# Whole PSUM pairs for every step of an attention and MLP kernel, and a fixed order per engine in the MLP

## The chip, the cores and the metric

The kernel runs on one core of a Trainium2 chip. The metric is device time in microseconds (us), the median of several executions; lower is better. One more execution of the kernel was profiled, and all rows below come from that one.

The engines are named as in the profile: PE (matrix multiply; PEld is its weight load), DVE, ACT, POOL, and SP, which issues the DMAs.

## The reference

Everything is float32 on the way out; the weights `w_ch1`, `w_ch2`, `U` and `V` of the second half come in as float64.

```python
# attention: batch 4, heads 12, seq 448, head_dim 64
scores = scale * q @ k^T                      # per head
scores = einsum('bhij,hg->bgij', scores, w_pre)    # mix the heads
attn = exp(scores - max); attn = attn / (sum + 1e-9)
attn = einsum('bhij,hg->bgij', attn, w_post)  # mix the heads again
x = (attn @ v) as (4, 448, 768)
# MLP: rank 32, d_ff 3072
h = x^T @ U @ V                               # along the sequence, low rank
u = x + h^T
out = u + max(u @ w_ch1, 0) @ w_ch2
```

## The kernel before

**Attention.** The tokens of a batch are cut into four groups (a unit `u` is one group of one batch, 16 in all), and each unit into chunks of ten tokens, 180 in all, taken in pairs `k`. The steps are `qk` (line 414), `premix` (445), `neg_max`, `exp`, `scale_w`, `postmix` (480), and, twice for each unit, `av` (521, 529). The result is added up in `acc[b]`, which holds batch b transposed: 6 chunks `c` of 128 channels by 448 tokens.

**Low rank.** When a batch is through, `flip` transposes its chunks (709), `flip_h` and `flip_l` take them out of PSUM as a high and a low part, `by_u` multiplies by U (727), `by_v` by V (740), and `add_h` adds the product to `acc[b]` (743). `split_uh` and `split_ul` then make `uh` and `ul`, the two parts of u that the MLP multiplies.

**MLP.** The hidden layer is cut into 24 slices `f` of 128. `up` (782) makes one slice for one batch: 18 matmuls (6 chunks, three products of high and low parts each) into one PSUM bank. `relu_h` (ACT, 787) and `relu_l` (DVE, 791) take it out as `hh` and `hl`. `down` (802) multiplies two slices at once by the second weights, six matmuls for each of the 6 chunks, each chunk into its own bank, and `gather` (DVE, 806) adds the bank to `acc[b]`. So a slice costs 4 x 18 matmuls up and 4 x 6 x 3 down, 144 in all.

**Weights.** Each slice has four pieces of 128x384 float64 words (two of each weight matrix). `piece` loads one (615) into one of two buffers `kr` and narrows it: `abs` (622 on ACT or 624 on DVE), then 629, 633, 634, 638 and 639 on DVE, the sum 643 on POOL or DVE, then the high part (a copy, on ACT, POOL or DVE) and the low part (a subtraction, line 339, on DVE or POOL). Each step is a step of the plan with a list of engines that may take it.

**What sets the order.** `Plan.order` is a list scheduler that runs when the kernel is built: each step has a rank (the table `RANK`), a cost, needs and slots; whenever an engine is free, it takes the ready step of lowest rank whose slots are free. What comes out is the program order of every engine. From slice 2 on (`RANK["even"]`), `plan.line` fixes the order of PE's MLP steps: one `up`, then three `down`s from a queue. The other engines' steps are ordered by rank alone.

**PSUM.** There are 8 banks, made as 4 tiles `BANKS[i]` of two banks each. The steps in `PAIRS` (`qk`, `pre`, `post`, `av`) take both halves of a tile; `lr` (low rank), `up` and `dn` take one half, and the other half may belong to another step at the same time:

```python
def bank(*s):
    w = plan.where[s]
    return BANKS[w[0] // 2] if len(w) == 2 else BANKS[w[0] // 2][:, w[0] % 2]
```

In the listings below the four tiles appear as bank_58 to bank_61, whichever half is meant.

Of the kernel before, what the change touches and what calls it, by code (L numbers as in the profile page):

```python
# [23 lines left out]
NJ = 4  # L24
# [21 lines left out]
class Unit:  # L46
# [11 lines left out]
    m0=7.312, mb=7.238, mf=2.802, e0=-51.192, estep=4.488, er=4.899, ne=8, qk_lead=5.047, qk_step=0.838, av_off=3.874,  # L58
    av_step=1.434, post=4.408, kr=3.969, vr=1.605, qr=5.01, mx=0.769, ex=1.029, ep=2.642, po=1.859, qo=0.493, 
    uv0=6, uvs=1.515, uv1=2.707, u0=0.057, us=8.218, w0=-3.04, w1=17.823, up=-0.049, raw=8, even=2, ga=-0.275, k0=-13.668, kstep=0.83,  # L60
# [3 lines left out]
CAPS = dict(qk=2, pre=3, post=3, av=2, lr=4, up=3, dn=6)  # L64
PAIRS = ("qk", "pre", "post", "av")
# [17 lines left out]
def f32(ap):  # L83
    return ap.bitcast(F32)
# [6 lines left out]
class Plan:  # L91
# [8 lines left out]
    def __init__(self, rings, banked, banks, weight):  # L100
        self.rings = {n: list(range(c)) for n, c in rings.items()}
        self.banked, self.where = banked, {}
        self.bank_free = list(range(banks))
        self.banks = banks
        self.weight = weight
        self.steps = {}
        self.port = {}
        self.users = {}
        self.line = []
# [20 lines left out]

    def fits(self, names):
        free = list(self.bank_free)
        for n in sorted(names, key=lambda n: n not in PAIRS):
            got = self.find(n, free)
            if got is None:
                return False
            for g in got:
                free.remove(g)
        return True

    def take(self, s):
        if s[0] not in self.banked:
            self.where[s] = self.rings[s[0]].pop(0)
            return
        got = self.find(s[0], self.bank_free)
        for g in got:
            self.bank_free.remove(g)
        if s[0] in PAIRS:
            self.pairs_left -= 1
        self.where[s] = got  # L150

    def order(self):
# [8 lines left out]
        self.pairs_left = sum(s[0] in PAIRS for s in self.users)  # L161
# [13 lines left out]
        place = {k: i for i, k in enumerate(self.line)}  # L175
        reached = 0

        def pick(e):
            for r in ready[e]:
                rank, _, k = r  # L180
                if place.get(k, reached) != reached:
                    continue
# [5 lines left out]
                if any(left[n] < c for n, c in need.items()) or not self.fits([n for n, c in need.items() if n in self.banked for _ in range(c)]):  # L188
                    continue
# [12 lines left out]
        while events:  # L202
            now = events[0][0]
            while events and events[0][0] <= now:
# [12 lines left out]
                for s in steps[k][4]:  # L217
                    users[s] -= 1
                    if users[s] == 0:
                        held.discard(s)  # L220
                        if s[0] in self.banked:
                            self.bank_free += self.where[s]
                        else:
                            self.rings[s[0]].append(self.where[s])
# [6 lines left out]
            while moved:  # L231
                moved = False
                for e in free:
# [7 lines left out]
                    reached += k in place  # L241
                    for o, _ in engines:
                        ready[o].remove(r)
                    for s in sorted(slots, key=lambda s: s[0] not in PAIRS):
# [30 lines left out]
def build(tc, q2, kt, vj, wpre_in, wpost_in, u_in, v_in, ident, w1j, w2, out, show=None):  # L275
# [11 lines left out]
    plan = Plan({**BUFS, **CAPS, "t": 2}, CAPS, 8, WEIGHT)  # L287
# [313 lines left out]
    def piece(key, src, n, p, rank, finish, slots, opened, cost, early=None):  # L601
# [57 lines left out]
        plan.add((key, "abs"), [("ACT", 60 + 395 * s), ("DVE", 60 + 210 * s)], narrow0, r0, [(key, 0)], [raw, first_tmp])  # L659
# [3 lines left out]
        plan.add((key, 4), [("POOL", 100 + 900 * s), ("DVE", 60 + 410 * s)], narrow4, r0, [(key, 3)], [first_tmp], port=BOTH)  # L663
# [42 lines left out]
    def flip(eng, b, c):  # L706
        t = T["tp", b, c] = bank("lr", ("tp", b, c))[:JP, :].rearrange("p (j c) -> p j c", j=NJ)
        for j in range(NJ):
            eng.transpose(t[:, j, :], acc[b][:, c, j * JP:(j + 1) * JP], sb["ident"])

    def flip_h(eng, b, c):
        xh = tile_of(("xh", b, c // 2), lambda: sb["xn"].tile([JP, NJ, LW], F32R, "xh", ("xn", (b, c // 2))))
        copy(eng, xh[:, :, c % 2 * 128:c % 2 * 128 + 128], T["tp", b, c])

    def flip_l(eng, b, c):
        xl = tile_of(("xl", b, c // 2), lambda: sb["xn"].tile([JP, NJ, LW], F32R, "xl", ("xn", (b, c // 2))))
        cut = slice(c % 2 * 128, c % 2 * 128 + 128)
        sub(eng, xl[:, :, cut], T.pop(("tp", b, c)), f32(T["xh", b, c // 2][:, :, cut]))

    def by_u(eng, b, k):  # L720
        xh, xl = T.pop(("xh", b, k)), T.pop(("xl", b, k))
        full = T["t1", b, k] = bank("lr", ("tr", b, k))
        ps = full[:, :LW]
        i = 0
        for y in (xl, xh):
            for j in range(NJ):
                eng.matmul(ps, lhsT=sb["u4"][:, j].rearrange("p i r -> p (i r)"), rhs=y[:, j, :], start=(i == 0), stop=(i == 7))
                i += 1

    def t_h(eng, b, k):  # L730
        t3 = T["t3", b, k] = sb["t3"].tile([4 * R, LW], F32R, "t3", ("t3", (b, k)))
        copy(eng, t3, T["t1", b, k][:, :LW])

    def t_l(eng, b, k):
        t3 = T["t3", b, k]
        sub(eng, t3[R:2 * R], T.pop(("t1", b, k))[R:2 * R, :LW], f32(t3[R:2 * R]))

    def by_v(eng, b, c):
        hp = T["hp", b, c] = bank("lr", ("hp", b, c))[:, :S]
        eng.matmul(hp, lhsT=T["t3", b, c // 2][:, c % 2 * 128:c % 2 * 128 + 128], rhs=sb["v4"], start=True, stop=True)  # L740

    def add_h(eng, b, c):
        eng.tensor_tensor(out=acc[b][:, c, :S], in0=acc[b][:, c, :S], in1=T.pop(("hp", b, c)), op=ALU.add)
# [7 lines left out]
    for b in range(B):  # L751
        RB = first[(b + 1) * NG] + RANK["uv0"]
        us = range(b * NG, (b + 1) * NG)
        for c in range(KC):
            k, r = c // 2, RB + RANK["uvs"] * c
            tp, xn = ("lr", ("tp", b, c)), ("xn", (b, k))
            plan.add(("tp", b, c), [("PE", 490)], partial(flip, b=b, c=c), r, ["ident"] + [("av_add", u, c // AV * AV) for u in us], [tp, xn])
            plan.add(("xh", b, c), [("ACT", 482)], partial(flip_h, b=b, c=c), r, [("tp", b, c)], [tp, xn])
            plan.add(("xl", b, c), [("DVE", 601)], partial(flip_l, b=b, c=c), r, [("xh", b, c)], [tp, xn])
        for k in range(KC // 2):  # L760
            r = RB + RANK["uvs"] * (2 * k + 1) + RANK["uv1"]
            tr, t3 = ("lr", ("tr", b, k)), ("t3", (b, k))
            plan.add(("t1", b, k), [("PE", 1450)], partial(by_u, b=b, k=k), r, [(("u",), 6), ("xl", b, 2 * k), ("xl", b, 2 * k + 1)], [tr, ("xn", (b, k))])
            plan.add(("th", b, k), [("ACT", 272)], partial(t_h, b=b, k=k), r, [("t1", b, k)], [tr, t3])
            plan.add(("tl", b, k), [("DVE", 336)], partial(t_l, b=b, k=k), r, [("th", b, k)], [tr, t3])
        for c in range(KC):
            k = c // 2
# [165 lines left out]
```

## Time and profile before

| | |
|---|---|
| median of 3 executions | 1213.48 us (1212.97 to 1216.55) |
| the profiled execution, its own time | 1214.14 us |
| its span, first to last instruction | 1212.3 us |
| PE busy | 1092.5 us, 90% of the span |
| DVE busy | 717.4 us, 59% |
| ACT busy | 379.9 us, 31% |
| POOL busy | 255.9 us, 21% |
| mean granted clock of PE | 0.961 of full speed |

About 1.8 us of the profiled execution's time lie outside its span. Matmuls are pipelined, so a busy share of PE counts overlapping instructions once and says little on its own; what one matmul costs is read from the distance between the starts of neighbours.

### The profile page before, as it was taken

How to read it: one execution, taken by the hardware profiler on the slowest of the kernel's cores; microseconds unless marked ns; L12 is line 12 of the kernel's file. 1: busy time of each engine (PE TensorE's matmuls, PEld its weight loads, DVE VectorE, ACT ScalarE, POOL GpSimd, SP SyncE). 2: the span in 40 equal slices, each digit the busy share in tenths (PEclk: the TensorE clock that was granted, in tenths of full speed). 3: DMA queues.
4: the chain of work that ended last, by engine and by line, in shares of the span. 5: the costliest groups of instructions: out<-in, count | busy, mean ns of one | idle time of the engine just before them, and what ended most of it. 6: DMA issues, size and time to landing. Idle time of an engine off the chain costs nothing.

```text
span 1212.3 us, 28459 instructions
## 1 busy us (share of the span) xinstructions
PE 1092.5 (90%) x12120; PEld 898.5 (74%) x12120; DVE 717.4 (59%) x1308; ACT 379.9 (31%) x811; POOL 255.9 (21%) x390
## 2 busy tenths in 40 slices
PE   4899999998999999988979888897988889798998
PEld 1556665666668888777868887786887778687897
DVE  0665654655887877565556465654646665565535
ACT  2767777677686222101101111110111011110100
POOL 3221111112145034121212121212212221221200
PEclk8999999999999999999989999997988999999899
DMA  7664555456642012111111111111101111111004
GB/s 274 193 195 151 172 184 162 146 157 201 195 147 75 27 52 79 52 53 26 53 49 43 40 52 52 42 37 52 52 27 52 53 40 39 52 53 31 22 1 182
DMA packets 52414, 108.11 MB, mean 89 GB/s; under 512 B 5200, under 2 KB 38464, under 8 KB 51776
## 3 DMA queue, kind: packets, MB, share of 16 engines
q1 hardware_dynamic: 52288, 106.30, 28.8%
q8 instruction: 95, 1.56, 0.5%
q14 instruction: 31, 0.25, 0.1%
HBM read 57.91 MB, written 7.08 MB: 54 GB/s over the span
## 4 chain that ended last, share of the span: by engine, by line
PE 70%; DVE 19%; DMA 4%; issue 3%; ACT 2%; SPq 1%; DVEq 0%; ACTq 0%; POOL 0%
PE bank L782 29%; PE bank L802 19%; PE bank L480 5%; PE bank L445 5%; DVE acc L806 5%; PE bank L414 5%; PE bank L521 5%; DMA t<-s 3%; DVE a L634 3%; DVE x L639 3%; DVE a L633 2%; DVE hl L791 2%; PE bank L529 1%; DVE w1l L339 1%; DVE x L638 1%
## 5 line engine op out<-in xcount | busy, mean ns | idle before, releaser
L782 PE MATMUL bank<-uh,w0l 128*128 128x448 f32 x576 | 227.9, 396 | 72.9 <-DVE acc L806 71.6
L787 ACT ACTIVATE hh<-bank 128x448 fp32r<-128x448 f32 x96 | 52.5, 547 | 647.2 <-PE bank L782 530.5
L806 DVE TENSOR_TENSOR acc<-acc,bank 128x448 f32<-128x448 f32 x300 | 181.2, 616 | 117.6 <-PE bank L782 74.1
L782 PE MATMUL bank<-ul,w0h 128*128 128x448 f32 x576 | 223.0, 387 | 0.0
L782 PE MATMUL bank<-uh,w0h 128*128 128x448 f32 x576 | 222.4, 386 | 0.0
L802 PE MATMUL bank<-hh,w1l 128*128 128x448 f32 x576 | 211.6, 367 | 4.0 <-DVE acc L806 3.0
L802 PE MATMUL bank<-hl,w1h 128*128 128x448 f32 x576 | 211.0, 366 | 0.3 <-DVE hl L791 0.2
L802 PE MATMUL bank<-hh,w1h 128*128 128x448 f32 x576 | 210.8, 366 | 0.0
L782 PEld LDWEIGHTS bank<-uh,w0l 128*128 128x128 f32 x576 | 116.8, 203 | 95.8 <-DVE acc L806 83.5
L643 POOL TENSOR_TENSOR a<-a,x 128x384 f32<-128x384 f32 (+2 forms) x97 | 102.3, 1055 | 392.3 <-DVE x L639 384.8
L791 DVE SCALAR_TENSOR_TENSOR hl<-bank,hh 128x448 fp32r<-128x448 f32 x96 | 59.4, 619 | 201.9 <-ACT hh L787 201.9
L450 DVE TENSOR_REDUCE mx<-bank 128x2 f32<-128x896 f32 x90 | 97.5, 1087 | 76.6 <-PE bank L445 71.5
L782 PEld LDWEIGHTS bank<-uh,w0h 128*128 128x128 f32 x576 | 116.6, 202 | 10.8
L782 PEld LDWEIGHTS bank<-ul,w0h 128*128 128x128 f32 x576 | 117.0, 203 | 10.1
L802 PEld LDWEIGHTS bank<-hh,w1l 128*128 128x128 f32 x576 | 108.1, 188 | 16.0 <-DVE acc L806 5.1
L455 ACT ACTIVATE e<-bank,mx 128x448 f32<-128x448 f32 x180 | 113.2, 639 | 20.8 <-DVE mx L450 11.5
L480 PEld LDWEIGHTS bank<-wr,e 60*64 60x64 f32 x5040 | 90.6, 136 | 37.1 <-issue 27.3
L802 PEld LDWEIGHTS bank<-hl,w1h 128*128 128x128 f32 x576 | 108.2, 188 | 10.0 <-DVE hl L791 0.9
L802 PEld LDWEIGHTS bank<-hh,w1h 128*128 128x128 f32 x576 | 108.2, 188 | 9.2
L414 PE MATMUL bank<-k,q 64*60 64x448 f32 (+1 forms) x768 | 95.3, 563 | 16.4 <-ACT s L332 9.6
L445 PE MATMUL bank<-t,wpre 64*64 64x448 f32 x720 | 90.3, 559 | 10.8 <-DMA t<-s 6.0
L480 PE MATMUL bank<-wr,e 60*64 60x60 f32 x5040 | 94.2, 220 | 6.0 <-issue 4.6
(64 smaller groups left out, 1122.0 us busy)
## 6 DMA issues: line engine op xcount, KB each, us to landing
t<-s SPq DMA_DIRECT2D x192, 210.0 KB
kr<-in_w1j SPq DMA_DIRECT2D x48, 384.0 KB
kr<-in_w SPq DMA_DIRECT2D x48, 384.0 KB
v<-in_vj SPq DMA_DIRECT2D x4, 1536.0 KB
q<-in_q SPq DMA_DIRECT2D x32, 186.0 KB
out<-acc SPq DMA_DIRECT2D x24, 224.0 KB
k<-in_kt SPq DMA_DIRECT2D x4, 672.0 KB
k<-in_kt SPq DMA_DIRECT2D x4, 448.0 KB
```

The costliest lines, as they stand in the source:

```text
L414: eng.matmul(o[at, i, :S], lhsT=q[d, p, at], rhs=k[d, p, :], start=True, stop=True)
L445: eng.matmul(o[64 * j:64 * j + 64, i, :S], lhsT=wpre[64 * i:min(64 * i + 64, QW)], rhs=tt[u % 2][64 * i:min(64 * i + 64, QW), n, :], start ...
L450: eng.tensor_reduce(out=mx, in_=T["pre", k][:, :, :S], axis=AX.X, op=ALU.max, negate=True)
L455: eng.activation(out=e[:, i], in_=T["pre", k][:, i, :S], func=ACTF.Exp, bias=T["mx", k][:, i:i + 1], accum_out=sm[:, i:i + 1])
L480: eng.matmul(d, lhsT=e[64 * j:64 * j + HALF, i, x * KB:x * KB + KB], rhs=wr[64 * j:64 * j + HALF, i].rearrange("p (g m) -> p g m", m=MH), ...
L521: eng.matmul(main[i * D:(i + 1) * D, c, :n], lhsT=v[:, p + c, i, x, :], rhs=a[:, x * H + 2 * (p + c) + i, :n], start=(c == 0 and x == 0), ...
L643: eng.tensor_tensor(out=f32(a), in0=f32(a), in1=f32(x), op=ALU.add)
L782: eng.matmul(ps, lhsT=w[:, c * 128:(c + 1) * 128], rhs=u[:, c, :], start=(i == 0), stop=(i == 3 * KC - 1))
L787: eng.activation(out=hh, in_=T["up", f, b], func=ACTF.Relu)
L791: eng.scalar_tensor_tensor(out=hl, in0=T.pop(("up", f, b)), scalar=0.0, in1=f32(T["hh", f, b]), op0=ALU.max, op1=ALU.subtract)
L802: eng.matmul(ps, lhsT=w[:, cut], rhs=h, start=(i == 0), stop=(i == len(todo) - 1))
L806: eng.tensor_tensor(out=dst, in0=dst, in1=T.pop(("dn", f, b, c)), op=ALU.add)
```

## The change

Every step that uses PSUM now takes a whole tile of two banks. `down`, the transposes and the V products work on two chunks per step, so that both banks are filled; `up` and the U products use the first bank of their tile and leave the second empty. The planner's search for halves (`find`, `fits`, `PAIRS`) goes. In the MLP, from slice 2 on, the order is fixed on four engines (`plan.lines`): for each batch b of slice f, the piece `(w, f + 1, b)` is narrowed, then `hh` and `hl` of `(f, b)`, then one `down` for an even b and two for an odd b, with their `gather`s. For pieces of slices above 2, `abs` and the high part are ACT's alone, the sum and the low part POOL's alone. The ranks are numbers of another search, of which two lines are shown.

```diff
 RANK = dict(
-    m0=7.312, mb=7.238, mf=2.802, e0=-51.192, estep=4.488, er=4.899, ne=8, qk_lead=5.047, qk_step=0.838, av_off=3.874,
+    m0=13.16, mb=7.238, mf=2.802, e0=-51.192, estep=4.488, er=6.178, ne=8, qk_lead=5.047, qk_step=0.838, av_off=4.137,
...
-CAPS = dict(qk=2, pre=3, post=3, av=2, lr=4, up=3, dn=6)
-PAIRS = ("qk", "pre", "post", "av")
+CAPS = dict(qk=2, pre=3, post=3, av=2, lr=2, up=2, dn=3)
...
     def take(self, s):
-        if s[0] not in self.banked:
-            self.where[s] = self.rings[s[0]].pop(0)
-            return
-        got = self.find(s[0], self.bank_free)
...
+        ring = self.bank_free if s[0] in self.banked else self.rings[s[0]]
+        self.where[s] = ring.pop(0)
...
-        place = {k: i for i, k in enumerate(self.line)}
-        reached = 0
+        place = {k: (n, i) for n, line in enumerate(self.lines) for i, k in enumerate(line)}
+        reached = [0] * len(self.lines)
...
-    plan = Plan({**BUFS, **CAPS, "t": 2}, CAPS, 8, WEIGHT)
+    plan = Plan({**BUFS, **CAPS, "t": 2}, CAPS, 4, WEIGHT)
...
     def bank(*s):
-        w = plan.where[s]
-        return BANKS[w[0] // 2] if len(w) == 2 else BANKS[w[0] // 2][:, w[0] % 2]
+        return BANKS[plan.where[s]]
...
-        plan.add((key, "abs"), [("ACT", 60 + 395 * s), ("DVE", 60 + 210 * s)], narrow0, r0, [(key, 0)], [raw, first_tmp])
+        plan.add((key, "abs"), [("ACT", 60 + 395 * s), ("DVE", 60 + 210 * s)][:1 if steady else 2], narrow0, r0, [(key, 0)], [raw, first_tmp])
...
-        plan.add((key, 4), [("POOL", 100 + 900 * s), ("DVE", 60 + 410 * s)], narrow4, r0, [(key, 3)], [first_tmp], port=BOTH)
+        plan.add((key, 4), [("POOL", 100 + 900 * s), ("DVE", 60 + 410 * s)][:1 if steady else 2], narrow4, r0, [(key, 3)], [first_tmp], port=BOTH)
...
-    def down(eng, fs, b, c):
-        cut = slice(c * 128, (c + 1) * 128)
-        ps = T["dn", fs[-1], b, c] = bank("dn", (fs[-1], b, c))[:, :S]
+    def down(eng, fs, b, c, n):
+        ps = T["dn", fs[-1], b, c] = bank("dn", (fs[-1], b, c))
...
-        for i, (w, h) in enumerate(todo):
-            eng.matmul(ps, lhsT=w[:, cut], rhs=h, start=(i == 0), stop=(i == len(todo) - 1))
-
-    def gather(eng, f, b, c):
-        dst = acc[b][:, c, :S]
-        eng.tensor_tensor(out=dst, in0=dst, in1=T.pop(("dn", f, b, c)), op=ALU.add)
...
+        for j in range(n):
+            for i, (w, h) in enumerate(todo):
+                eng.matmul(ps[:, j, :S], lhsT=w[:, (c + j) * 128:(c + j + 1) * 128], rhs=h, start=(i == 0), stop=(i == len(todo) - 1))
+
+    def gather(eng, f, b, c, n):
+        eng.tensor_tensor(out=two(b, c, n), in0=two(b, c, n), in1=T.pop(("dn", f, b, c))[:, :n, :S], op=ALU.add)
...
-                  [(f"w{i // 2}", f)], "open_a" if i > 1 else ("open_qk", "open_mix", "open_a")[min(f, 2)], (HIGH(HW), LOW(HW)), early() if f < 2 else None)
+                  [(f"w{i // 2}", f)], "open_a" if i > 1 else ("open_qk", "open_mix", "open_a")[min(f, 2)], ([("ACT", act(HW))], [("POOL", gps(HW))]) if f > RANK["even"] else (HIGH(HW), LOW(HW)),
+                  early() if f < 2 else None, f > RANK["even"])
...
-                line.append(("up", f, b))
-                line += queue[:3]
-                del queue[:3]
...
+    def some(n):
+        lines["PE"] += [("dn",) + q for q in queue[:n]]
+        lines["DVE"] += [("ac",) + q for q in queue[:n]]
+        del queue[:n]
+
+    for f in range(RANK["even"], KF):
         for b in range(B):
...
+            lines["PE"].append(("up", f, b))
+            key = ("w", f + 1, b)
+            if f + 1 < KF:
+                lines["ACT"].append((key, "abs"))
+                lines["DVE"] += [(key, i) for i in (1, 2, 3)]
+                lines["POOL"] += [(key, i) for i in (4, 6)]
+            lines["ACT"].append(("hh", f, b))
+            lines["DVE"].append(("hl", f, b))
+            if f + 1 < KF:
+                lines["ACT"].append((key, 5))
+            some(1 + b % 2)
+            queue += [(f, b, c) for c in range(KC) if ("dn", f, b, c) in plan.steps]
+    some(len(queue))
```

What this does to PE's order is seen from the tile that each group of matmuls writes. The rows below are the first matmul of each group, from the middle of the MLP of the kernel before; a group of line 802 (a `down`) has 6 matmuls, one of line 782 (an `up`) has 18.

```order
L802 MATMUL bank_61<-hh_6245,w1l_6326 128x448
...
L802 MATMUL bank_58<-hh_6245,w1l_6326 128x448
...
L802 MATMUL bank_60<-hh_6245,w1l_6326 128x448
...
L782 MATMUL bank_58<-uh,w0l_5888 128x448
...
L802 MATMUL bank_61<-hh_6245,w1l_6326 128x448
...
L802 MATMUL bank_60<-hh_6245,w1l_6326 128x448
...
L802 MATMUL bank_59<-hh_6245,w1l_6326 128x448
...
L782 MATMUL bank_59<-uh,w0l_5888 128x448
```

The first `up` goes into tile 58, whose other half the `down` before last has just filled; the second goes into tile 59, whose other half the `down` right ahead of it has filled. In the changed kernel PE's row in the middle of the MLP reads as follows, again the first matmul of each group; a group of line 770 (a `down`) now has 12 matmuls, one of line 750 (an `up`) has 18.

```order
L770 MATMUL bank_58<-hh_6034,w1l_6279 128x448
...
L770 MATMUL bank_61<-hh_6034,w1l_6279 128x448
...
L750 MATMUL bank_60<-uh,w0l_5825 128x448
...
L770 MATMUL bank_59<-hh_6200,w1l_6279 128x448
...
L750 MATMUL bank_58<-uh,w0l_5825 128x448
...
L770 MATMUL bank_61<-hh_6200,w1l_6279 128x448
...
L770 MATMUL bank_60<-hh_6200,w1l_6279 128x448
...
L750 MATMUL bank_59<-uh,w0l_5825 128x448
```

Each tile now comes back after exactly three other groups. The second place is DVE in the same stretch. Before, two pieces are narrowed with their instructions mixed, then `hl` and the `gather`s (`acc`) follow in the order of their ranks:

```order
L633 SCALAR_TENSOR_TENSOR a_5404<-kr_545,a_5404 128x384
L634 SCALAR_TENSOR_TENSOR a_5404<-x_5403,a_5404 128x384
L638 TENSOR_SCALAR x_599<-a_600 128x384
L639 SCALAR_TENSOR_TENSOR x_599<-kr_732,x_599 128x384
L638 TENSOR_SCALAR x_5403<-a_5404 128x384
L639 SCALAR_TENSOR_TENSOR x_5403<-kr_545,x_5403 128x384
L791 SCALAR_TENSOR_TENSOR hl_6079<-bank_59,hh_6051 128x448
L806 TENSOR_TENSOR acc<-acc,bank_61 128x448
L806 TENSOR_TENSOR acc<-acc,bank_58 128x448
L806 TENSOR_TENSOR acc<-acc,bank_60 128x448
L791 SCALAR_TENSOR_TENSOR hl_5990<-bank_58,hh_5978 128x448
```

In the changed kernel DVE's row has one piece, one `hl` (line 759) and one or two `gather`s (line 773), each of two chunks, and then the next piece:

```order
L759 SCALAR_TENSOR_TENSOR hl_5959<-bank_58,hh_5956 128x448
L773 TENSOR_TENSOR acc<-acc,bank_61 128x2x448
L773 TENSOR_TENSOR acc<-acc,bank_60 128x2x448
L596 TENSOR_SCALAR a_600<-kr_765 128x384
L600 SCALAR_TENSOR_TENSOR a_600<-kr_765,a_600 128x384
L601 SCALAR_TENSOR_TENSOR a_600<-x_599,a_600 128x384
L605 TENSOR_SCALAR x_599<-a_600 128x384
L606 SCALAR_TENSOR_TENSOR x_599<-kr_765,x_599 128x384
L759 SCALAR_TENSOR_TENSOR hl_6202<-bank_59,hh_6200 128x448
```

No two pieces stand one behind the other any more, and no `gather` or `hl` reads a tile that another open step shares.

## Rows read from the trace of the kernel before

**Rows 1.** PE in three stretches (stretch, length, busy, instructions, clock, DMA share, GB/s).
```profile
370.33:476.43 106.10, 98.50 (x695) 1.00 0.20 58
476.43:1183.71 707.28, 636.49 (x2932) 0.95 0.15 43
542.34:1102.72 560.38, 500.18 (x2304) 0.95 0.16 46
```

**Rows 2.** The chain that ended last (start, length, what): groups of 18 matmuls.
```profile
683.14 5.50 PE bank L782 x18
688.64 3.65 PE bank L802 x18
...
1144.15 3.72 PE bank L802 x18
```

**Rows 3.** Who waited for whom, whole span (total us, times, longest).
```profile
ACT hh L787 <- DVE acc L806: 114.6, 19, 6.6
DVE acc L806 <- PE bank L782: 74.1, 19, 4.3
PE bank L782 <- DVE acc L806: 71.6, 30, 3.7
```

**Rows 4.** Timeline of one stall: DVE, then ACT, POOL and PE (in brackets: idle before, and its releaser).
```profile
676.21 0.62 DVE L806 TENSOR_TENSOR acc<-acc,bank 128x448 f32<-128x448 f32 x1 [3.70 <-PE bank L782]
680.26 1.23 DVE L639 SCALAR_TENSOR_TENSOR x<-kr,x 128x384 f32<-128x384 uint32 x1
681.41 0.61 DVE L791 SCALAR_TENSOR_TENSOR hl<-bank,hh 128x448 fp32r<-128x448 f32 x1
681.95 1.67 DVE L806 TENSOR_TENSOR acc<-acc,bank 128x448 f32<-128x448 f32 x3
...
680.03 1.04 POOL L643 TENSOR_TENSOR a<-a,x 128x384 f32<-128x384 f32 x1 [11.21 <-DVE x L639]
...
683.14 0.47 PE L782 MATMUL bank<-uh,w0l 128*128 128x448 f32 x1 [3.32 <-DVE acc L806]
```

**Rows 5.** Groups of instructions in the stretch 542.34 to 1102.72 (busy, mean ns, idle before).
```profile
L782 PE MATMUL bank<-uh,w0l 128*128 128x448 f32 x384 | 154.0, 401 | 60.2 <-DVE acc L806 60.2
...
L806 DVE TENSOR_TENSOR acc<-acc,bank 128x448 f32<-128x448 f32 x193 | 116.8, 615 | 84.4 <-PE bank L782 63.8 <-PE bank L802 20.1
...
L802 PEld LDWEIGHTS bank<-hh,w1h 128*128 128x128 f32 x384 | 72.1, 188 | 6.0
...
L643 POOL TENSOR_TENSOR a<-a,x 128x384 f32<-128x384 f32 x64 | 69.1, 1080 | 289.5 <-DVE x L639 289.5
L639 DVE SCALAR_TENSOR_TENSOR x<-kr,x 128x384 f32<-128x384 uint32 x64 | 46.7, 730 | 2.2
L634 DVE SCALAR_TENSOR_TENSOR a<-x,a 128x384 f32<-128x384 f32 x64 | 45.6, 712 | 5.9 <-DVE a L633 0.5
L633 DVE SCALAR_TENSOR_TENSOR a<-kr,a 128x384 int32<-128x384 int32 x64 | 35.4, 553 | 0.5
...
L638 DVE TENSOR_SCALAR x<-a 128x384 int32<-128x384 int32 x64 | 22.5, 352 | 0.0
L629 DVE TENSOR_SCALAR a<-kr 128x384 int32<-128x384 int32 x64 | 21.2, 353 | 0.0
```

**Rows 6.** The group over the whole span in which DVE reads two PSUM banks at once.
```profile
L450 DVE TENSOR_REDUCE mx<-bank 128x2 f32<-128x896 f32 x90 | 97.5, 1087 | 76.6 <-PE bank L445 71.5 <-ACT e L455 4.8
```

**Rows 7.** Timeline: two weight loads of SP's queue, and the ACT step that waited for them.
```profile
437.62 1.85 SPq L615 DMA_DIRECT2D kr<-in_w1j  x2
...
442.49 0.56 ACT L622 ACTIVATE x<-kr 128x384 f32<-128x384 f32 x1 [2.23 <-DMA kr<-in_w1j]
```

**Rows 8.** Timeline: `hh` and `hl` after the `up` that ended at 668.71.
```profile
668.96 0.55 ACT L787 ACTIVATE hh<-bank 128x448 fp32r<-128x448 f32 x1 [7.54 <-PE bank L782]
...
669.53 0.62 DVE L791 SCALAR_TENSOR_TENSOR hl<-bank,hh 128x448 fp32r<-128x448 f32 x1 [3.24 <-ACT hh L787]
```

**Rows 9.** Busy time of all engines from 390 to 480 us (PE, PEld, DVE, ACT, POOL, clock, DMA).
```profile
390.00:480.00 90.00, 82.40 (x412) 73.64 (x411) 70.87 (x132) 22.37 (x44) 23.24 (x22) 1.00 0.18 49
```

More of the change, by code (lines that the diff above doesn't have):

```diff
@@ L180, in pick @@
                 rank, _, k = r
-                if place.get(k, reached) != reached:
+                if k in place and place[k][1] != reached[place[k][0]]:
                     continue
@@ L187, in pick @@
                         need[s[0]] = need.get(s[0], 0) + 1
-                if any(left[n] < c for n, c in need.items()) or not self.fits([n for n, c in need.items() if n in self.banked for _ in range(c)]):
+                if any(left[n] < c for n, c in need.items()) or sum(c for n, c in need.items() if n in self.banked) > len(self.bank_free):
                     continue
@@ L599, in build, with piece @@
     count = [0]
-    def piece(key, src, n, p, rank, finish, slots, opened, cost, early=None):
+    def piece(key, src, n, p, rank, finish, slots, opened, cost, early=None, steady=False):
         count[0] += 1
@@ L731, in t_h, with by_v, two, add_h @@
         t3 = T["t3", b, k] = sb["t3"].tile([4 * R, LW], F32R, "t3", ("t3", (b, k)))
-        copy(eng, t3, T["t1", b, k][:, :LW])
+        copy(eng, t3, T["t1", b, k])
     def t_l(eng, b, k):
         t3 = T["t3", b, k]
[L736 to L743, printed above, removed]
+        sub(eng, t3[R:2 * R], T.pop(("t1", b, k))[R:2 * R], f32(t3[R:2 * R]))
+    def by_v(eng, b, k):
+        hp = T["hp", b, k] = bank("lr", ("hp", b, k))
+        for i in range(2):
+            eng.matmul(hp[:, i, :S], lhsT=T["t3", b, k][:, i * 128:(i + 1) * 128], rhs=sb["v4"], start=True, stop=True)
+    def two(b, c, n=2):
+        return acc[b][:, c:c + n, :S]
+    def add_h(eng, b, k):
+        eng.tensor_tensor(out=two(b, 2 * k), in0=two(b, 2 * k), in1=T.pop(("hp", b, k))[:, :, :S], op=ALU.add)
     def split_uh(eng, b, c):
@@ L753, in build @@
         us = range(b * NG, (b + 1) * NG)
[L754 to L759, printed above, removed]
@@ L850, in build @@
                 if f == KF - 1:
-                    plan.add(("out", b, c), [("SP", (480, 640))], partial(store, b=b, c=c), r, [("ac", f, b, c)])
+                    plan.add(("out", b, c), [("SP", (480, 640 * n))], partial(store, b=b, c=c, n=n), r, [("ac", f, b, c)])
             last[b] = f
-    queue, line = [], []
-    for f in range(KF):
-        for b in range(B):
-            if f >= RANK["even"]:
-                line.append(("up", f, b))
-                line += queue[:3]
-                del queue[:3]
-            if ("dn", f, b, 0) in plan.steps and f >= RANK["even"]:
-                queue += [("dn", f, b, c) for c in range(KC)]
@@ L863, in build @@
-    line += queue
-    plan.line = line
+    queue = []
+    lines = {e: [] for e in ("PE", "ACT", "DVE", "POOL")}
+    plan.lines = list(lines.values())
+    def some(n):
[3 more added lines that the diff above has]
+    for f in range(RANK["even"], KF):
+        for b in range(B):
+            lines["PE"].append(("up", f, b))
[10 more added lines that the diff above has]
+            queue += [(f, b, c) for c in range(KC) if ("dn", f, b, c) in plan.steps]
```

113 lines of the change are left out of this document (45 added, 68 removed).

## The prediction

> **What bounds the kernel now.** I read the busy time by stage first, then the waits, then the timeline of one wait. From 476.43 to 1183.71 us, the part of the MLP in which the order of PE is fixed, PE runs 2932 matmuls in 707.28 us [rows 1], 0.241 us each. The chain of waits shows what a matmul costs when nothing is in its way: 18 of them in 3.65 us in most groups, 3.72 us in others, 0.2028 and 0.2067 us each [rows 2]. I don't know what tells the two paces apart; about two thirds of the undisturbed groups have the shorter. At these paces the stretch needs 594.6 to 606.0 us, so 101 to 113 us of it are lost. The other engines are not full: the loss is waiting.
>
> The list of waits names the place. PE's first matmul of an `up` waited 71.6 us in 30 waits for a `gather` on DVE; DVE's `gather` waited 74.1 us in 19 waits for an `up`; ACT's `hh` waited 114.6 us for a `gather` [rows 3]. In the 16 slices from 542.34 to 1102.72, 60.2 us of PE's idle time stand before that first matmul and next to nothing elsewhere [rows 5]. The rest of the loss there is 560.38 - 60.2 = 500.2 us for 2304 matmuls that need 467 to 476 us: 24 to 33 us go at a lower clock. The granted clock of that stretch is 0.95 [rows 1], and an `up` after a long wait takes 5.50 us where the next group takes 3.65 [rows 2].
>
> One stall, step by step [rows 4]. The third `gather` of a round starts at 676.21, after 3.70 us of idle DVE, and what released it is an `up`, not its own `down`. The order before shows why: that `up` writes the other half of the tile from which this `gather` reads. The halves hold different steps' data, but the wait goes by the tile. Behind this `gather` stand, in DVE's order, the rest of two pieces of weights, an `hl` and three more `gather`s; they run up to 683.62. PE has finished its three `down`s 3.32 us before 683.14, at 679.82, and wants to start an `up` in a tile whose other half waits for the second of these `gather`s. It starts at 683.14. This returns about three times (3.3, 3.7, 0.5 us) in each two slices.
>
> **The change part by part.**
>
> *Whole tiles.* No two steps share a tile, so a `gather` waits for its own `down` alone, `hh` and `hl` for their own `up`, and an `up` for the step that held its tile last. In the new order of PE three other groups lie between two uses of a tile: 18 + 12 + 12 matmuls at least, 42 x 0.2028 = 8.5 us. So a tile is missed only when DVE empties it more than 8.5 us after the matmuls that filled it have ended.
>
> *How late DVE empties.* `hh` starts 0.25 us after its `up` ends and `hl` 0.57 us after that [rows 8]: the tile of an `up` ending at T is free at T + 1.4 if DVE is there. The `down` behind it ends at T + 2.4 (12 x 0.2028), a second one at T + 4.9. The two-chunk `gather` has no row. Above, it is two of today's, 2 x 0.615 = 1.23 us [rows 5]; below, half the elements would be 0.62; a DVE instruction that reads 896 elements from PSUM takes 1.087 us [rows 6], and I take 1.09. It then ends at T + 3.7, or T + 6.2 after two. The next piece takes 0.353 + 0.553 + 0.712 + 0.352 + 0.730 = 2.70 us [rows 5], and is through at T + 6.4, or T + 8.9. The next `up` ends at T + 6.1, or T + 8.5, and its `hl` could start 0.8 later. So DVE is back in time at every step; what waits behind a `gather` on DVE (piece, `hl`) is then not late for PE, and a tile is emptied within about 2 us of the 8.5.
>
> *DVE's load.* Two steps of PE are 72 matmuls, 14.7 us at 0.204. DVE has in them two pieces (5.40), two `hl` at 0.61 [rows 4] and three `gather`s (3.27 to 3.69): 9.9 to 10.3 us, 70%. The low parts that DVE did before are gone from it.
>
> *ACT and POOL alone.* The sum on POOL takes 1.08 us [rows 5] and a low part about the same by that row, 2.2 us for each step of 7.35: no bound. ACT has three instructions of at most 0.55 us for each step. Their cover is the piece's lead: piece `(w, f + 1, b)` is narrowed a slice before PE needs it. With that cover gone PE would wait some 4 us per piece (sum, copy, difference, hand-offs).
>
> *Loads of weights.* Their number and size stay; SP moves past no other queue in the MLP. A buffer `kr` is free again when its piece is narrowed, and is wanted one other piece later, about 12 us by the timetable above. Two loads issued at 437.62 had the ACT step behind them started at 442.49 [rows 7], 4.9 us: hidden. The DMA engines are 15% busy [rows 1].
>
> *Attention, low rank, start, end.* Nearly the same order of the same matmuls; two-chunk transposes save a dozen hand-offs for each batch, off PE's path. At the start one load of k goes behind one of q, which may cost some tenths. The new ranks I take as 0, with 6 us either way: from 370 to 476 PE is busy 98.5 of 106.1 us [rows 1], some 8 us to win or to double. The end (the last `down` of one chunk, its `gather`, its store) stays.
>
> **Sum.** For 2932 matmuls I take 0.204 us, between the two paces and nearer the more frequent: 598 us in place of 707, so -109 (bounds -113 and -101). The profiled execution took 1214.14 us, 1.8 more than its span and 0.7 more than the median shown. 1214.1 - 109 = **1105 us**, 9% less.
>
> **The rivals.**
>
> *A. As above*: 1094 to 1117 us (the bounds -113 and -101, with 6 for the rest and some tenths at each seam). For it: near the end, once the last pieces are through DVE, today's order already runs at 0.2067 us a matmul [rows 2], although the halves are still shared.
>
> *B. DVE stays the bound.* POOL now runs all sums and low parts while DVE narrows. A row shows what that can do: line 639 took 1.23 us at 680.26 while POOL's 643 ran from 680.03 on, against 0.55 for an undisturbed instruction of that shape (line 633's mean) [rows 4, 5]. With all three such instructions at 1.23 a piece is 4.40 us and two steps of DVE 8.8 + 1.2 + 3.7 = 13.7 us, still under 14.7. It decides from 4.9 us a piece on; at 5.5 us, two steps are 15.9 and 42 of them cost 1.2 x 42 = 50 us: 1155. The Trainium skill ("SBUF — State Buffer", Who interferes with whom) says that a DVE instruction with two SBUF inputs and a GpSimd instruction that reads SBUF lock each other out for a whole instruction, whichever comes first. By that rule, as an estimate, DVE loses at most POOL's two instructions, 2.2 us a piece, 4.9 with the 2.70, which is just where it begins to decide: the rule speaks against the change, and the row of 680.26 agrees with its form. Against B: by the timetable POOL's low part falls where DVE waits for `hl` or `gather`.
>
> *C. Slower: the four fixed rows turn as one loop.* ACT's `abs` of a piece stands behind the high part of the piece before, that behind POOL's sum, that behind DVE's narrowing, that behind its `abs`. The loop is 0.55 + 2.70 + 1.08 + 0.55 and four hand-offs of up to 0.25 us: 5.9 us, under the step of 7.35. If the `hh` that stands in ACT's row and the `hl` and `gather`s in DVE's stretch it, every step takes the loop's time. Today's step, 560.38 us / 64 = 8.76 [rows 1], is where the change becomes a loss; at 9.2 us the 84 steps with pieces give 1214 + 84 x 0.44 = 1251.
>
> *D. The start of the MLP gets worse.* From 390 to 480 DVE is 79% busy (70.87 of 90 us) [rows 9]: there it has the low-rank step, `ul` and four pieces of slice 2 at once, and the new order puts four `up`s in a row there, each with a whole tile. If PE waits 12 to 25 us more there, the steady part still gains: 1117 to 1130.
>
> *E. More than the rows' pace.* If matmuls came as fast as the weight loads, 188 ns [rows 5], the stretch would take 551 us: 1058. No undisturbed group has come under 0.2025. The Trainium skill ("TensorE: Matmul & The Clock Gate", Back-to-back issue gap) gives N / 2.4 + 2.5 ns, an estimate of 189 ns for 448 columns, and 1062 us; the rows differ from it and decide.
>
> **How the numbers follow.** A 0.75, B 0.10, C 0.05, D 0.09, E 0.01. The predicted time is A's. The range must leave out no more than 0.2: 1094 (A's lower end) to 1128, into D. A measurement of this kernel can tell about 0.3%, 3.6 us. A, D, E and nearly all of B are faster: 0.94; C is slower: 0.05; B with a piece so slow that it eats all of the gain: 0.01 for no change.
>
> **What would show it.** Right: PE's idle time before an `up` falls from 72 us to under 10, the granted clock of the steady part goes to 0.99 or more, a slice takes 29 to 30 us, and the two-chunk `gather` reads about 1.1 us with a `down` as its releaser. Wrong: PE waits for `gather` or `hl` still, with pieces of 4.9 us or more on DVE (B); ACT's high part or DVE's line 596 waiting at each step, PE idle before `up` for weights (C); idle PE between 380 and 490 (D). The forecast fails above all if the releaser of DVE's waits was not the shared tile but DVE's own order, or if PE's pace in a long dense run is another one than in the short ones of before.

## The result, and the profile after

The changed kernel takes 1089.91 us (median of 4 executions, 1086.06 to 1100.28), the kernel before, on the same chip, 1215.01: a ratio of 0.898, interval 0.891 to 0.905. The change is faster by 10%, the direction forecast, but the median is 15 us below the 1105 forecast and 4 below the range's lower end of 1094. The profiled execution is the slowest of the four: 1100.28 us, span 1098.5.

The same counts of matmuls as in [rows 1], in the changed kernel's trace (stretch, length, busy of PE, PEld, DVE, ACT, POOL, clock, DMA share, GB/s):

```profile
0.00:367.26 367.26, 331.50 (x8379) 213.59 (x8379) 216.10 (x357) 257.14 (x556) 83.09 (x212) 0.98 0.57 180
367.26:464.60 97.34, 97.34 (x695) 88.48 (x695) 70.19 (x106) 28.64 (x54) 27.16 (x28) 1.00 0.19 54
464.60:1070.24 605.64, 605.64 (x2932) 550.12 (x2931) 366.26 (x600) 122.07 (x241) 161.65 (x160) 1.00 0.18 51
1070.24:1098.50 28.26, 24.58 (x119) 21.98 (x118) 13.97 (x16) 0.54 (x1) 0.00 (x0) 1.00 0.52 195
```

The 695 matmuls that took 106.10 us take 97.34, the 2932 that took 707.28 take 605.64, and in both PE is busy from the first to the last moment: length and busy time are the same number, and the clock is 1.00. The attention ends 3.1 us earlier (367.26 against 370.33), the last stretch is the same to 0.3 us (28.26 against 1212.3 - 1183.71 = 28.59). The difference is -101.6 in the part with the fixed order, -8.8 at the start of the MLP, -3.1 in the attention, -0.3 at the end: -113.8, the difference of the two spans.

The groups from 544.10 to 1020.26 (the 16 slices from slice 6 on; busy, mean ns of one, idle before and its releaser), to be held against [rows 5]:

```profile
L750 PE MATMUL bank<-uh,w0l 128*128 128x448 f32 x384 | 141.3, 368 | 0.0
...
L773 DVE TENSOR_TENSOR acc<-acc,bank 128x896 f32<-128x896 f32 x96 | 104.5, 1089 | 124.7 <-PE bank L770 124.7
...
L610 POOL TENSOR_TENSOR a<-a,x 128x384 f32<-128x384 f32 x64 | 64.9, 1014 | 306.5 <-PE bank L750 302.6 <-DVE x L606 3.9
...
L601 DVE SCALAR_TENSOR_TENSOR a<-x,a 128x384 f32<-128x384 f32 x64 | 35.8, 559 | 7.1 <-DVE a L600 0.5
L606 DVE SCALAR_TENSOR_TENSOR x<-kr,x 128x384 f32<-128x384 uint32 x64 | 35.7, 559 | 2.2
```

The 60.2 us of idle PE before an `up` are 0.0. The two-chunk `gather` takes 1.089 us and now waits for a `down` (line 770), in no case for an `up`. In the list of waits the three lines of [rows 3] are gone; in their places stand:

```profile
ACT hh L755 <- PE bank L750: 312.2, 52, 8.1
DVE acc L773 <- PE bank L770: 172.9, 137, 1.4
DVE hl L759 <- ACT hh L755: 81.3, 91, 3.3
```

`hh` and `gather` wait for the matmuls that they read, and `hl` waits for its `hh`. The chain that ended last is PE alone in this stretch (start, length, what):

```profile
702.98 4.96 PE bank L770 x24
707.94 3.72 PE bank L750 x18
711.66 2.48 PE bank L770 x12
714.14 3.72 PE bank L750 x18
```

And DVE and POOL beside it, one odd step (timeline):

```profile
703.65 0.62 DVE L759 SCALAR_TENSOR_TENSOR hl<-bank,hh 128x448 fp32r<-128x448 f32 x1 [0.74 <-ACT hh L755]
705.50 1.09 DVE L773 TENSOR_TENSOR acc<-acc,bank 128x896 f32<-128x896 f32 x1 [1.23 <-PE bank L770]
707.98 1.09 DVE L773 TENSOR_TENSOR acc<-acc,bank 128x896 f32<-128x896 f32 x1 [1.39 <-PE bank L770]
708.98 0.36 DVE L596 TENSOR_SCALAR a<-kr 128x384 int32<-128x384 int32 x1
...
711.02 0.56 DVE L606 SCALAR_TENSOR_TENSOR x<-kr,x 128x384 f32<-128x384 uint32 x1
...
702.98 1.02 POOL L610 TENSOR_TENSOR a<-a,x 128x384 f32<-128x384 f32 x1 [3.55 <-PE bank L750]
704.63 1.01 POOL L306 TENSOR_TENSOR w0l<-a,w0h 128x384 fp32r<-128x384 f32 x1 [0.63 <-ACT w0h L299]
```

An `up` ends at 702.98 and its tile is empty at 704.27, 1.3 us later. The two `down`s behind it end at 705.46 and 707.94 and are emptied 1.1 us later each. The piece is through at 711.58, just before the next `up` ends at 711.66. DVE has waits of 0.7, 1.2 and 1.4 us in between: it waits for PE, not the other way round. POOL's two instructions for a piece lie at 702.98 and 704.63, ahead of the piece that DVE narrows from 708.98 on.

### The profile page after: what moved, and what is told of

Read it like the earlier page. It is cut to its first block, busy times and chain, and to the rows that moved or that the text cites. A ratio compares the mean times of both kernels' runs of the same rounds, so it can differ in the third digit from the quotient of the medians.

```text
span 1098.5 us, 28397 instructions
## 1 busy us (share of the span) xinstructions
PE 1059.1 (96%) x12120; PEld 874.2 (80%) x12120; DVE 666.5 (61%) x1076; ACT 408.4 (37%) x852; POOL 271.9 (25%) x398
## 4 chain that ended last, share of the span: by engine, by line
PE 89%; DMA 4%; ACT 3%; DVE 2%; issue 2%; SPq 0%; POOL 0%; ACTq 0%; DVEq 0%
PE bank L750 33%; PE bank L770 33%; PE bank L447 6%; PE bank L488 5%; PE bank L381 5%; PE bank L412 5%; DMA t<-s 3%; ACT e L422 2%; PE bank L496 1%; DVE mx L417 1%; PE bank L677 1%; PE bank L694 1%; ACT s L299 1%; DMA k<-in_kt 0%; ACT a L299 0%
## 5 line engine op out<-in xcount | busy, mean ns | idle before, releaser
L773 DVE TENSOR_TENSOR acc<-acc,bank 128x896 f32<-128x896 f32 (+1 forms) x153 | 163.5, 1070 | 173.5 <-PE bank L770 172.9
L750 PE MATMUL bank<-uh,w0l 128*128 128x448 f32 x576 | 212.2, 368 | 0.0
L750 PE MATMUL bank<-uh,w0h 128*128 128x448 f32 x576 | 211.9, 368 | 0.0
L750 PE MATMUL bank<-ul,w0h 128*128 128x448 f32 x576 | 211.9, 368 | 0.0
L610 POOL TENSOR_TENSOR a<-a,x 128x384 f32<-128x384 f32 (+2 forms) x98 | 98.6, 1006 | 422.6 <-PE bank L750 381.2
L750 PEld LDWEIGHTS bank<-uh,w0l 128*128 128x128 f32 x576 | 108.1, 188 | 10.9
L750 PEld LDWEIGHTS bank<-uh,w0h 128*128 128x128 f32 x576 | 108.1, 188 | 10.9
L750 PEld LDWEIGHTS bank<-ul,w0h 128*128 128x128 f32 x576 | 108.1, 188 | 10.8
L381 PE MATMUL bank<-k,q 64*64 64x448 f32 (+1 forms) x768 | 96.1, 569 | 15.5 <-ACT s L299 9.0
L412 PE MATMUL bank<-t,wpre 64*64 64x448 f32 x720 | 87.6, 557 | 8.8 <-DMA t<-s 5.8
```

Source lines behind the costliest of these rows:

```text
L381: eng.matmul(o[at, i, :S], lhsT=q[d, p, at], rhs=k[d, p, :], start=True, stop=True)
L412: eng.matmul(o[64 * j:64 * j + 64, i, :S], lhsT=wpre[64 * i:min(64 * i + 64, QW)], rhs=tt[u % 2][64 * i:min(64 * i + 64, QW), n, :], start ...
L610: eng.tensor_tensor(out=f32(a), in0=f32(a), in1=f32(x), op=ALU.add)
L750: eng.matmul(ps, lhsT=w[:, c * 128:(c + 1) * 128], rhs=u[:, c, :], start=(i == 0), stop=(i == 3 * KC - 1))
L773: eng.tensor_tensor(out=two(b, c, n), in0=two(b, c, n), in1=T.pop(("dn", f, b, c))[:, :n, :S], op=ALU.add)
```

## The experiments

Each kernel's table row is from its own profiled execution, except for the median and the ratio to the kernel before on the same chip (with its 95% interval; that kernel took 1221.50 us beside e1 to e4 and 1218.31 beside e5 to e8). "Start" is the time of the first `up`, "24 ups" the time from there to the first `up` of slice 6, "two slices" the mean time of two slices over the 16 slices that follow. Two slices are 288 matmuls: 58.4 us at 0.2028 us a matmul, 59.5 at 0.2067.

| kernel | median us | ratio | start | 24 ups | two slices |
|---|---|---|---|---|---|
| before | 1215.01 | | 370.26 | 202.1 | 70.05 |
| changed | 1089.91 | 0.898 [0.891, 0.905] | 367.20 | 176.9 | 59.52 |
| e1 whole tiles, PE's order alone | 1087.77 | 0.892 [0.885, 0.899] | 367.35 | 174.3 | 58.37 |
| e2 halves, order on four engines | 1121.35 | 0.921 [0.915, 0.927] | 371.79 | 190.3 | 59.73 |
| e3 before, up apart from down | 1123.05 | 0.921 [0.914, 0.929] | 376.03 | 198.6 | 58.99 |
| e4 changed, old ranks | 1097.28 | 0.902 [0.895, 0.910] | 373.49 | 175.6 | 58.37 |
| e5 changed again | 1090.90 | 0.896 [0.892, 0.899] | 370.66 | 174.3 | 58.37 |
| e6 changed, two tiles | 1089.39 | 0.894 [0.891, 0.897] | 371.52 | 174.3 | 58.37 |
| e7 before, new ranks | 1162.63 | 0.953 [0.950, 0.957] | 376.22 | 191.0 | 64.04 |
| e8 changed, forced waits | 1118.18 | 0.917 [0.913, 0.921] | 368.85 | 174.4 | 61.18 |

**e1: whole tiles without the fixed order of ACT, DVE and POOL.** The changed kernel with the order fixed on PE alone, and every piece's steps free again to choose their engine:

```diff
-        plan.add((key, "abs"), [("ACT", 60 + 395 * s), ("DVE", 60 + 210 * s)][:1 if steady else 2], narrow0, r0, [(key, 0)], [raw, first_tmp])
+        plan.add((key, "abs"), [("ACT", 60 + 395 * s), ("DVE", 60 + 210 * s)], narrow0, r0, [(key, 0)], [raw, first_tmp])
...
-        lines["DVE"] += [("ac",) + q for q in queue[:n]]
...
-            if f + 1 < KF:
-                lines["ACT"].append((key, "abs"))
-                lines["DVE"] += [(key, i) for i in (1, 2, 3)]
-                lines["POOL"] += [(key, i) for i in (4, 6)]
-            lines["ACT"].append(("hh", f, b))
-            lines["DVE"].append(("hl", f, b))
-            if f + 1 < KF:
-                lines["ACT"].append((key, 5))
```

> The changed kernel with the fixed order on PE alone: ACT, DVE and POOL choose by rank again and may share the weight steps as before, but every step holds a whole tile. If the shared tile was the cause of the stalls, they stay away although DVE narrows two pieces in a row again: three other groups (8.5 us) lie between two uses of a tile, and two pieces take 5.4 us. Then PE is idle under 10 us in the steady MLP and the time is 1085 to 1105 us. If the fixed order on DVE was what mattered, some 30 to 70 us of idle PE come back: 1125 to 1170 us.

The same time as the changed kernel within what can be told, and a PE without idle time (stretches from the start and from slice 6):

```profile
367.35:541.65 174.30, 174.30 (x1086) 160.85 (x1079) 133.75 (x214) 43.63 (x83) 51.91 (x54) 1.00 0.21 62
541.65:1008.59 466.94, 466.94 (x2305) 432.81 (x2304) 307.24 (x529) 72.98 (x144) 116.90 (x128) 1.00 0.19 55
```

Whole tiles, with the ranks and PE's order that came with them, bring all of the gain. The order on the other engines is not needed for it. It does change DVE: line 601 takes 715 ns here in the mean and 559 in the changed kernel:

```profile
L601 DVE SCALAR_TENSOR_TENSOR a<-x,a 128x384 f32<-128x384 f32 x64 | 45.7, 715 | 5.6
```

The mean hides two lengths. Of the 64, 48 take 0.56 us, and the 16 that run beside a sum on POOL (line 610) take 1.18 to 1.19, for example:

```profile
573.56 1.18 DVE L601 SCALAR_TENSOR_TENSOR a<-x,a 128x384 f32<-128x384 f32 x1
...
573.06 1.26 POOL L610 TENSOR_TENSOR a<-a,x 128x384 f32<-128x384 f32 x1 [5.93 <-DVE x L606]
```

**e2: the fixed order without whole tiles.** The kernel before, halves and single chunks as they were, with the lines on four engines and the fixed choice of engines:

```diff
+            lines["PE"].append(("up", f, b))
...
+                lines["DVE"] += [(key, i) for i in (1, 2, 3)]
...
+            lines["DVE"].append(("hl", f, b))
...
+            some(3)
```

> The kernel before with the fixed order on all four engines (one up, then three one-chunk downs per step), halves of tiles shared as before. In its order of PE a down in the other half of an up's tile comes directly behind that up in every second step, so if the wait goes by the tile, that down waits for hl, about 1.4 us, and a down two places behind another up about 0.2 us: 1.6 x 42 two-steps = 70 us of idle PE before line 803, and 1150 to 1180 us. If the order was what mattered, PE is dense: 1085 to 1110 us.

Both forecasts missed: 1121 lies between. From slice 6 on two slices take 59.73 us, 1.4 more than the 58.37 of e1 at the same pace, so with one piece, one `hl` and the `gather`s in turn the shared tiles cost PE little, although they are still shared: some 0.35 us in each second step, before a `down` two places behind an `up`. The 1.4 us of waiting forecast for the `down` right behind an `up` did not come, because the coupling there runs the other way: in the program that `down` stands ahead of the `up`'s `hh`, so `hh` waits for the `down` that fills the other half of its tile. Over the whole run (total us, times, longest):

```profile
ACT hh L788 <- PE bank L803: 279.1, 41, 8.4
```

That wait is on ACT, off PE's path. What is left is at the start of the MLP, 190.3 us where whole tiles take 174 to 177:

```profile
442.00 0.47 PE L803 MATMUL bank<-hh,w1l 128*128 128x448 f32 x1 [1.65 <-DVE acc L807]
455.20 0.47 PE L803 MATMUL bank<-hh,w1l 128*128 128x448 f32 x1 [1.67 <-DVE acc L807]
471.91 0.47 PE L803 MATMUL bank<-hh,w1l 128*128 128x448 f32 x1 [1.86 <-DVE acc L807]
```

**e3: no tile shared between an up and a down.** The kernel before; `up` takes halves of one tile alone, `down` those of the other three, order by rank as before:

```diff
+        if name in ("up", "dn"):
+            free = [i for i in free if (i < 2) == (name == "up")]
         if name in PAIRS:
```

> The kernel before with one rule more for the halves: up only in tile 58, down only in the other three, so that no up shares a tile with a down; one-chunk steps and the order by rank stay. If the shared tile is the cause, DVE's gather no longer waits for an up (74 us before, under 15 now) and most of the 72 us of idle PE go: 1095 to 1125 us. If it is DVE's order or the double work per instruction, the time stays above 1180 us.

58.99 us for two slices, and 0.6 us of idle PE before an `up` where it was 60.2 [rows 5] (groups from 574.60 to 1046.49):

```profile
L784 PE MATMUL bank<-uh,w0l 128*128 128x448 f32 x385 | 142.3, 370 | 0.6 <-DVE hl L793 0.3
```

The stalls of the steady part are gone with nothing else changed but who shares a tile with whom: from slice 6 on PE, DVE, ACT and POOL run the same instructions in the same order as in the kernel before. So a stall of the steady part needs a tile that an `up` shares with a `down`. Whether the order on DVE alone would remove it with the halves as they were is not shown, since e2 moved the halves as well: there, as in e7 below, an `up` shares its tile with a `down` behind it. At the start two `up`s now share a tile and wait for each other's `hl`:

```profile
409.01 0.74 PE L784 MATMUL bank<-uh,w0l 128*128 128x448 f32 x1 [4.08 <-DVE hl L793]
...
477.21 0.74 PE L784 MATMUL bank<-uh,w0l 128*128 128x448 f32 x1 [4.00 <-DVE hl L793]
```

**e4 and e7: the ranks.** e4 is the changed kernel with the table `RANK` of before, e7 the kernel before with the table of the change; nothing else differs. The cut shows the first line of three, for e4; e7's edit is the reverse.

```diff
-    m0=13.16, mb=7.238, mf=2.802, e0=-51.192, estep=4.488, er=6.178, ne=8, qk_lead=5.047, qk_step=0.838, av_off=4.137,
+    m0=7.312, mb=7.238, mf=2.802, e0=-51.192, estep=4.488, er=4.899, ne=8, qk_lead=5.047, qk_step=0.838, av_off=3.874,
...
```

> The changed kernel with the rank table of before. The steady MLP is the same; what differs is attention and the start of the MLP. If the new ranks brought the 9 us between the first up and the steady part, PE is idle 6 to 10 us there again and the time is 1094 to 1104 us at the pace of the fast executions; if whole tiles brought it, there is next to no idle time and 1086 to 1094 us.

> The kernel before with the changed kernel's table of ranks and nothing else: tiles are still shared. Theory (the ranks bring some 6 us in the attention, by the run of the changed kernel with the old ranks, and the dense start of the MLP comes from the whole tiles): 1200 to 1215 us beside a kernel before of about 1215, PE's waits behind gather still over 50 us, idle PE between 380 and 480 us still over 4 us. Rival (the ranks make the start dense too): idle PE between 380 and 480 us falls under 1.5 us.

e4: the start and the steady part are as dense with the old ranks (175.6, 58.37). The first `up` starts at 373.49 in place of 367 to 371.5. So PE's missing idle time came as forecast for whole tiles, and the time, 1097, as forecast for the ranks, but from the later start. The median is 7 us above the changed kernel's; the intervals overlap, so the size of what the ranks bring on whole tiles is not settled.

e7 is a miss: 1163 us, when I expected no less than 1200 (the idle PE between 380 and 480 us, 5.6 us, is as expected). On shared halves the ranks alone are worth 4.7%. Most of it lies in the steady part, 64.04 us for two slices in place of 70.05; the 24 `up`s take 11 us less, and the first `up` starts 6 us later than before. PE's waits there (groups from 567.26 to 1079.56):

```profile
L802 PE MATMUL bank<-hh,w1l 128*128 128x448 f32 x384 | 147.0, 383 | 27.3 <-DVE hl L791 18.0 <-DVE acc L806 5.4
```

27 us before a `down`, most of it in waits of about 0.6 to 1.3 us, where before it was 60.2 us before an `up`, up to 3.7 at a time; and the clock is 1.00 there. The ranks reach into PSUM: the planner hands out the halves in the order in which its model frees them, and with the new numbers an `up` falls into other halves. Nothing else differs from slice 6 on, where the order of PE, DVE, ACT and POOL is that of the kernel before. In PE's row of e7, in the middle of the MLP, first matmul of each group, an `up`'s neighbour is a `down` behind it, not the one ahead of it:

```
L782 MATMUL bank_60
L802 MATMUL bank_61
L802 MATMUL bank_60
L802 MATMUL bank_61
L782 MATMUL bank_59
L802 MATMUL bank_58
L802 MATMUL bank_59
L802 MATMUL bank_58
```

So how much a shared tile costs depends on which steps happen to share it; with whole tiles that question is gone, and the ranks matter little.

**e5: the changed kernel again.**

> The changed kernel once more, unchanged. Theory (the matmuls come at one of two paces, 0.2028 or 0.2067 us, and a stretch without any wait keeps the one it began with): the times fall in two groups, about 1086 to 1088 and about 1100, with little between except where the pace changes half way; the profiled execution shows one pace from about 410 us to the end, 58.4 us or 59.5 us for each two slices. Rival (the spread of 1086 to 1100 is something else, for example the attention): two slices take the same in every profiled execution and the first up starts earlier or later by 10 us or more.

The profiled execution (1090.45 us) is at the shorter pace throughout, 58.37 us for two slices:

```profile
370.66:466.60 95.94, 95.94 (x699) 88.21 (x693) 70.15 (x107) 28.74 (x55) 26.94 (x28) 1.00 0.19 56
466.80:1061.60 594.80, 594.80 (x2937) 551.17 (x2936) 366.85 (x600) 121.11 (x241) 162.00 (x160) 1.00 0.18 52
```

But the six times (1086.47, 1089.21, 1090.45, 1091.36, 1095.84, 1097.28) do not fall in two groups, and here the first `up` starts 3.4 us later than in the profile after. So both the theory and its rival hold a part: between the two profiled executions the pace accounts for about 13 us and the attention for 3.4 the other way, 9.8 together, as measured (1100.28 and 1090.45). What spreads the other executions is not shown, since they have no profile.

**e6: two tiles in place of four.** From slice 4 on `up` and `down` use only two tiles:

```diff
+        self.where[s] = ring.pop(ring.index(self.room(s)[0]) if s[0] in self.banked else 0)
+
+    def room(self, s):
+        return [i for i in self.bank_free if s[0] not in ("up", "dn") or s[1][0] < 4 or i < 2]
...
```

> The changed kernel, but up and down use only two of the four tiles from slice 4 on, still one step to a tile. One other group then lies between two uses of a tile, at least 12 matmuls, 2.43 us. The trace of the changed kernel shows a tile empty 1.5 us after its up has ended (hl ends at 704.27 for an up that ended about 702.8) and 1.3 us after its down. Theory (what cost time was that two steps shared a tile, not the number of tiles; the 8.5 us of reserve are not needed): the same time as the changed kernel, 1086 to 1100 us, PE's idle time behind DVE under 5 us. Rival (the reserve is what absorbs a late DVE, when a piece of weights stands ahead of an hl): waits of 1 to 2 us behind hl or gather at one place in each slice or more, 20 to 60 us in all, 1110 to 1150.

The theory's case: 1089.39 us, and no idle PE from slice 6 on:

```profile
545.83:1012.77 466.94, 466.94 (x2305) 432.81 (x2304) 291.91 (x480) 96.37 (x192) 129.89 (x128) 1.00 0.18 55
```

The 8.5 us between two uses of a tile, on which the prediction rested its first step, are more than three times what is needed: 2.4 us (12 matmuls) are enough where a tile is emptied after 1.1 to 1.3.

**e8: waits put back.** The changed kernel, but from slice 5 on all `down`s of batch 0 use tile 0:

```diff
+        one = s[0] == "dn" and s[1][0] > 4 and s[1][1] == 0
+        return [i for i in self.bank_free if not one or i == 0]
...
```

> The changed kernel, but from slice 5 on the three downs of batch 0 all use the same tile; two of them follow each other directly, so PE waits once in each two slices for a gather, 10 times in all. Price by the rows of the changed kernel: the gather starts 0.2 us after the down ends and takes 1.09, so 1.3 to 1.6 us a wait, 13 to 16 us in all. Theory (a wait lets the pace be drawn anew, mostly 0.2028): after each wait the pace is one of the two, 0.2028 more often, so that a profiled execution that is at 0.2067 before the first wait leaves it; 1098 to 1108 us. Rival (the pace is a property of the execution): one pace throughout, whatever the waits, and with 0.2067 1112 to 1118. If a wait also costs a lower granted clock, as in the kernel before (5.50 us for 18 matmuls in place of 3.65), each wait costs 1.8 us more, and the sum is 18 higher.

1118, ten above the forecast's upper end, because there are two waits in each two slices, not one: a `down` also meets tile 0 while it holds an `up`.

```profile
622.72 0.47 PE L774 MATMUL bank<-hh,w1l 128*128 128x448 f32 x1 [1.29 <-DVE hl L763]
632.68 0.48 PE L774 MATMUL bank<-hh,w1l 128*128 128x448 f32 x1 [1.18 <-DVE acc L777]
```

They cost 61.39 - 58.37 = 3.0 us in each full two slices (the first `up` of slice 8 starts at 603.02, that of slice 10 at 664.41), 1.5 each, as priced: the idle time of 1.2 to 1.3 and 0.3 of restart. The clock stays at 1.00, so waits of this length cost nothing by a lower clock. Of the eighteen restarts sixteen take up 0.2028; those of 1052 and 1091 run at 0.2067. The pace is not a property of the execution: it can change at a wait.

## Why the prediction was right, and where it failed

**The mechanism was right.** The waits went by the tile: separating `up` from `down` alone (e3) removes them from the steady part with every engine's order unchanged, and putting waits back (e8) costs 1.5 us for each. The low clock of the middle (0.95) went with the stalls, as the term of 24 to 33 us supposed: it is 1.00.

**The steps of DVE's timetable were right.** The prediction had the two `gather`s end at T + 3.7 and T + 6.2 and the piece at T + 8.9; with T = 702.98 they end at 3.61, 6.09 and 8.60. The `gather` was taken at 1.09 and takes 1.089. A slice takes 29.8 us, forecast 29 to 30.

**The step that failed: "The new ranks I take as 0, with 6 us either way."** It held the start of the MLP too. I read there that PE was busy 98.5 of 106.1 us and called it some 8 us to win or to double, and then booked nothing, as if the steady part's cause did not act there. It does. In the kernel before, for example, this `up` waits for the `hl` of the `up` in the other half of its tile:

```profile
461.46 0.47 PE L782 MATMUL bank<-uh,w0l 128*128 128x448 f32 x1 [1.25 <-DVE hl L791]
```

Most of the waiting at the start of e2 and e3 is for `gather` and `hl`, and with whole tiles (changed, e1, e4, e5, e6) the start is dense with either table of ranks. The 695 matmuls took 8.8 us less in the profiled execution and about 11 at the shorter pace (e5: 699 in 95.94, so 695 in about 95.4). The name "ranks" was wrong as well: they alone bring the 24 `up`s from 202 to 191 us, whole tiles with old ranks to 175.6.

**A size that was off: the pace.** For 2932 matmuls I took 0.204 us. The profiled execution runs at 0.2066 (605.64 / 2932), 7.5 us more than the 598 forecast; e5's at 0.2025 (594.80 / 2937), 4.3 less, at the edge of my bounds. The sum closes for both profiled executions: 1105 - 8.8 + 7.5 - 3.1 (attention) - 0.3 (end) = 1100.3 beside 1100.28, and 1105 - 10.7 - 4.3 + 0.4 (attention) = 1090.4 beside e5's 1090.45. The profiles of e1, e4, e5 and e6 have the shorter pace too, so the median of 1089.9 probably goes with it; its own executions have no profile. The range reached to -113 for the pace and -6 for the rest, and so ended where the start's 11 begin to count. The profiled execution, 1100.28, lies inside the range only because its longer pace takes back most of what the start gained.

**The rivals.** B (DVE bound by POOL) did not come: a piece takes 0.355 + 0.559 + 0.559 + 0.361 + 0.559 = 2.39 us on DVE, less than the 2.70 assumed and half the 4.9 at which it decides. In the fixed order POOL's sum and low part run ahead of the piece on DVE, not beside it, and lines 601 and 606 take 559 ns against 712 and 730 before [rows 5]. Those means hide two lengths, as in e1: in the kernel before 48 of the 64 instructions of either line take 0.56 us, and the 16 beside a sum on POOL 1.16 to 1.26. In the changed kernel none of the 64 runs beside POOL. The Trainium skill ("SBUF — State Buffer", Who interferes with whom) says that a DVE instruction with two SBUF inputs contends with a GpSimd instruction that reads SBUF. The two lengths agree with it, but the time so saved was not on PE's path. C (the four rows as one slow loop) did not come, since every engine but PE has waits left over. D had the sign of the start wrong. E's 188 ns did not come either.

## What to carry to other kernels

When waits go by a tile, give a tile to one step at a time before adding more buffers: here two whole tiles from slice 4 on did as well as four, and taking `up` and `down` out of common tiles alone was worth 8%. A cause found in the steady part should be looked for, and booked, in the ramp ahead of it too. Before moving a scheduler's numbers, look at which steps they put into a common tile: on shared halves the numbers alone moved the time by 4.7%.

## What was not expected of the hardware

Dense matmuls with a weight load each come at one of two paces here, and without a wait the `up`s and `down`s keep their pace for hundreds of microseconds (the changed kernel 0.2067 from 409 to 1070 us, e5 0.2025 from 467 to 1062). PEld in the changed kernel's profiled execution, 500 to 1050 us (busy, mean ns, idle before):

```profile
L770 PEld LDWEIGHTS bank<-hh,w1h 128*128 128x128 f32 x444 | 83.4, 188 | 8.4
```

and in e1's:

```profile
L770 PEld LDWEIGHTS bank<-hh,w1h 128*128 128x128 f32 x452 | 84.9, 188 | 6.7
```

The load takes 188 ns in both; the gap ahead of it is 8.4 / 444 = 19 ns in the one and 6.7 / 452 = 15 in the other. Over the 3456 matmuls of the MLP these 4 ns are 13 us, 1.2% of the time, with the granted clock at 1.00 in both. The Trainium skill ("TensorE: Matmul & The Clock Gate", Back-to-back issue gap) gives N / 2.4 + 2.5 ns for a single matmul by itself, an estimate of 189 ns for 448 columns. No 18 neighbours in any run came under a mean of 202 ns, and the measurement decides. What sets the pace is open. e8 shows that it can change at a wait, and a wait is not needed: in the profile after, the matmuls of line 770 from 401 to 405 us come at 0.203, and from 406 us, behind eight matmuls by U (line 694) and with no idle time between, at 0.207.
